# Moving a normalising multiply to GpSimd and charging more transfers in a build-time schedule

## The chip, the cores and the metric

The kernel runs on one core of a Trainium2 chip. The metric is the device time in microseconds (us) of one execution. The profile also gives a span, from the first to the last instruction, which here is about 1.8 us shorter than the time. A run also has a mean granted clock of TensorE, 1.0 being full speed.

The engines: TensorE (PE in the profile) multiplies matrices, ScalarE (ACT) evaluates exponentials, VectorE (DVE) and GpSimd (POOL) do elementwise work, SyncE (SP) issues transfers (DMA).

## The reference, cut to what matters

Two identical layers on an input of 2048 rows and 512 columns in bfloat16. Attention has 32 heads of size 16, so the number of exponentials is large against the size of the matrix products; the feed-forward part has 1792 hidden columns.

```python
def _A_ref(x, wqkv, wo):                      # attention
    ...
    scores = einsum("bhqd,bhkd->bhqk", q, k) * Dh ** -0.5     # 32 heads, 2048 x 2048 each
    p = softmax(scores)
    o = einsum("bhqk,bhkd->bhqd", p, v)
    return o.reshape(B, S, D) @ wo

x = x + _A_ref(layernorm(x), wqkv, wo)
x = x + silu(layernorm(x) @ w1) @ w2
# ... and both lines once more
```

## The kernel before

The kernel is one long stream. In each step TensorE makes four blocks of scores of 128x512 (128 keys by 512 queries). ScalarE takes the exponential of three of them (one instruction on 128x1024, tile `s_ps`, and one on 128x512). The fourth block, `d_ps`, is turned into an exponential without ScalarE: VectorE scales it into 16-bit integers `d_y` that are read as fp16 numbers, and GpSimd adds two offsets to a pair of such blocks, giving `d_z`. Then TensorE multiplies probabilities with values. `d_ps` has one PSUM buffer, so a late evacuation by VectorE holds up the next step's scores, and so ScalarE.

All other work (projections, layernorm, transposes by DMA, feed-forward, head outputs) is background work. It is fitted into the stream when the program is built, by a small model of the engines' clocks:

```python
class Model:
    EXP1 = 0.48          # exponential of 128x512
    EXP2 = 0.905         # of 128x1024
    TRANSPOSE = 1.27     # what one DMA transpose occupies of the queue
    TRANSPOSED = 1.7     # from there until the model counts it as landed
    DMA = 0.64           # what one plain load occupies of the queue
    ...
    def pool_busy(self, us):
        self.pool = max(self.pool, self.dve + 0.1) + us
        return self.pool + 0.1
    def transpose(self):
        self.sp = max(self.sp, self.dve + 0.1) + self.TRANSPOSE
        self.landed = self.sp + self.TRANSPOSED
    def fits(self, cost, landed=0.0):
        held, pe, dve, sums, _ = cost
        if landed > (self.pe if pe else self.dve):
            return False
        ...
```

A part of background work is put in where `fits` says yes; engines then execute in that order whatever the real times are. If the model believes a transfer has landed and it has not, the engine that waits for it holds up everything behind it in its queue.

The output of a head is normalised at its end. For 45 of 64 groups it comes by a DMA transpose (`ot`), for the other 19 through TensorE and PSUM (`att`). Both are then multiplied by the reciprocal of the sums on VectorE:

```python
nc.vector.reciprocal(rec[:], att[:, :, :, 16:17])
yield part(0.43, held=not by_dma(L, qc, pi, g, par))   # the model charges 0.43 us
nc.vector.tensor_tensor(out=attn[...], in0=att[:, :, :, 0:DH],
                        in1=rec[:].to_broadcast([P, 4, 4, DH]), op=ALU.mult)
```

The layernorm result `xn` is also made on VectorE, one 128x513 piece at a time, and transposed by DMA (`xnT`, `fT`):

```python
nc.vector.tensor_scalar(out=wide..., in0=x_wide[...], scalar1=mv[:, 0:1], scalar2=rstd,
                        op0=ALU.subtract, op1=ALU.mult)
```

Before the stream lies a prologue of 14 us (load, layernorm of the first rows, first projection), behind it a tail of 41 us.

The softmax here doesn't subtract the row's maximum and nothing guards it: scores larger than these inputs give would overflow.

## Time and profile before

Three runs took 1565.21 to 1566.28 us, median 1565.61 us. The first view is the one of the cores, the second the head of the page (busy time of each engine, its share of the span, number of instructions).

```profile
core 0: 1562.4 us, clock 0.993
```

```profile
span 1562.4 us, 34354 instructions
PE 1474.8 (94%) x13400; PEld 468.1 (30%) x13400; DVE 1079.3 (69%) x1733; ACT 1513.8 (97%) x2191; POOL 1114.4 (71%) x1184
```

ScalarE is the bound. An exponential of 128x1024 that follows directly behind another instruction ends 0.917 us after it, one of 128x512 0.490 us after it. 1026 + 1032 + 98 (the tanh of the feed-forward) of them make about 1495 us. The stream ran from 14.12 to 1521.5 us. So ScalarE lost only some 13 us inside the stream. (Lost time is counted here from the end of one exponential to the end of the next, less 0.917 or 0.490 us; the cut-off for small waits moves a trace's sum by about 0.4 us. The mean durations in the views below are longer than these figures, because the records of exponentials that follow each other overlap.) It follows that no change that leaves the exponentials alone can win more than these and a little of the prologue.

| where ScalarE waited in the trace of before | us |
|---|---|
| start of the stream, 30 to 45 us | 3.0 |
| 86 us | 1.5 |
| 253 to 256 us | 4.1 |
| 239, 269, 457, 554, 644, 1053 to 1055, 1207 us, each about 3 to 3.5 us behind the start of a slow head-output multiply | 3.5 |
| small ones | 1.0 |

The groups of instructions by shape show the work in question (columns: busy us, mean ns of one; then idle time before them and what ended it).

```profile
L1157 ACT ACTIVATE p_sb<-s_ps 128x512 bf16<-128x512 f32 x1013 | 901.6, 890 | 9.3 <-PE d_ps L925 8.2 <-PE s_ps L925 1.1
L619 DVE TENSOR_TENSOR attn<-ot,rec 128x256 bf16<-128x256 bf16 x45 | 49.4, 1098 | 1.5
L619 DVE TENSOR_TENSOR attn<-att,rec 128x256 bf16<-128x256 f32 x19 | 8.0, 421 | 0.4
L414 DVE TENSOR_SCALAR xn<-x,mv,rstd 128x513 bf16<-128x513 bf16 x64 | 41.6, 663 | 5.7 <-DMA fT<-xn 4.3 <-POOL rstd L408 1.3
```

The same multiply takes 421 ns when its data is in PSUM (`att`) and 1098 ns when both inputs are in SBUF (`ot`), and the model charges 0.43. The timeline shows one of them (start us, duration us, engine, line, instruction; in brackets the idle time before and what ended it).

```profile
453.63 1.04 POOL L1094 TENSOR_SCALAR d_z_7582<-d_y 128x1024 uint16<-128x1024 uint16 x1 [1.39 <-DVE rec L617]
453.67 1.28 DVE L619 TENSOR_TENSOR attn<-ot,rec 128x256 bf16<-128x256 bf16 x1
454.87 0.67 DVE L668 SCALAR_TENSOR_TENSOR hT<-t_sb,h_ps 128x512 bf16<-128x512 f32 x1
...
455.69 0.59 PE L480 MATMUL h_ps<-fT,w_7504 128*128 128x512 bf16 x2 [1.31 <-DVE hT L668]
...
456.68 1.51 ACT L1157 ACTIVATE p_sb<-s_ps 128x512 bf16<-128x512 f32 x2 [0.42 <-PE d_ps L925]
```

The multiply starts 0.04 us after a GpSimd `d_z` and is held until that ends; the evacuation `hT` behind it is late, TensorE waits 1.31 us for it, and ScalarE in the end loses 0.42 us. The largest single loss has another cause, a transfer that landed late:

```profile
246.69 5.58 SPq L317 DMA_TRANSPOSE fT<-xn  x3
...
250.63 0.42 DVE L414 TENSOR_SCALAR xn<-x,mv,rstd 128x513 bf16<-128x513 bf16 x1 [4.13 <-DMA fT<-xn]
...
251.70 0.37 PE L925 MATMUL d_ps<-QT,KT 32*128 32x512 bf16 x1 [3.15 <-DVE d_y L1074]
...
253.44 1.51 ACT L1157 ACTIVATE p_sb<-s_ps 128x512 bf16<-128x512 f32 x2 [3.00 <-PE d_ps L925]
```

VectorE stood 4.13 us in front of an `xn` whose buffer was still being read by an earlier transpose; `d_y` stood behind it, the next `d_ps` behind that, and ScalarE waited 3.00 us.

### The profile page before, as it was taken

The numbers are of one execution on the slowest core, as the hardware profiler recorded it, in microseconds if no ns is written. First come the engines' busy times: TensorE is split into PE (matmuls) and PEld (weight loads), VectorE is DVE, ScalarE is ACT, GpSimd is POOL, SyncE is SP. The second block draws the span as 40 slices with busy tenths as digits, with TensorE's granted clock in tenths as the row PEclk, the third lists the DMA queues.
The fourth block names the chain that finished last, engine by engine and source line by source line (L and its number), as shares of the span: only waits on it lengthen the run. The fifth ranks groups of instructions, "written<-read, shape, count | busy, mean of one in ns | idle before, by whom it ended". The sixth has DMA issues, their size and how long they took to land. (4 is left out here: it accounts for less than half of the span.)

```text
span 1562.4 us, 34354 instructions
## 1 busy us (share of the span) xinstructions
PE 1474.8 (94%) x13400; PEld 468.1 (30%) x13400; DVE 1079.3 (69%) x1733; ACT 1513.8 (97%) x2191; POOL 1114.4 (71%) x1184
## 2 busy tenths in 40 slices
PE   7999998899999999899998999998999899999998
PEld 3222332232322322222322323322332232222225
DVE  6877676667776777767776677676667666676645
ACT  6999998999999999999999999999999999999993
POOL 2888776677876778667876778776777677776760
PEclk9999999999999999999999999999999999999999
DMA  4110023101221112201122010121022101121110
GB/s 142 28 28 2 5 39 62 31 18 42 45 45 28 31 25 49 52 17 41 21 47 45 11 35 8 25 58 32 18 46 62 30 19 29 45 48 22 39 45 14
DMA packets 149443, 55.85 MB, mean 36 GB/s; under 512 B 127776, under 2 KB 148768, under 8 KB 149280
## 3 DMA queue, kind: packets, MB, share of 16 engines
q1 hardware_dynamic: 149280, 53.65, 15.0%
q8 instruction: 105, 1.72, 0.5%
q14 instruction: 58, 0.48, 0.1%
HBM read 28.57 MB, written 4.19 MB: 21 GB/s over the span
## 5 line engine op out<-in xcount | busy, mean ns | idle before, releaser
L1157 ACT ACTIVATE p_sb<-s_ps 128x512 bf16<-128x512 f32 x2026 | 1468.6, 1105 | 9.3 <-PE d_ps L925 8.2
L1074 DVE TENSOR_SCALAR d_y<-d_ps 128x512 uint16<-128x512 f32 x1012 | 696.9, 689 | 400.5 <-PE d_ps L925 359.5
L925 PE MATMUL s_ps<-QT,KT 32*128 32x512 bf16 x3084 | 629.8, 383 | 51.6 <-ACT p_sb L1157 38.8
L925 PE MATMUL d_ps<-QT,KT 32*128 32x512 bf16 x1012 | 390.1, 385 | 10.3 <-DVE d_y L1074 7.1
L925 PEld LDWEIGHTS <-KT 32*128 32x128 bf16 x4096 | 186.8, 91 | 639.9 <-issue 587.1
L949 PE MATMUL o_ps<-p_sb,VA 128*32 128x512 bf16 x3039 | 311.8, 388 | 8.2 <-DVE oB L1054 1.1
L949 PE MATMUL o_ps<-d_y,VA 128*32 128x512 f16 x1012 | 153.2, 379 | 0.0
L949 PEld LDWEIGHTS <-VA 128*32 128x32 bf16 x4096 | 86.7, 95 | 161.6 <-issue 123.8
L727 PE MATMUL f_ps<-w_sb,hT 128*128 128x512 bf16 x392 | 104.1, 382 | 0.0
L949 PEld LDWEIGHTS <-VB 128*32 128x32 f16 x2024 | 78.3, 98 | 55.6 <-issue 0.8
L949 PE MATMUL o_ps<-w_qkv,zero 128*32 128x512 bf16 x1344 | 93.1, 382 | 0.0
L665 ACT ACTIVATE t_sb<-h_ps 128x512 f32<-128x512 f32 x98 | 88.1, 899 | 0.0
L668 DVE SCALAR_TENSOR_TENSOR hT<-t_sb,h_ps 128x512 bf16<-128x512 f32 x98 | 67.2, 686 | 22.8 <-ACT t_sb L665 22.6
L619 DVE TENSOR_TENSOR attn<-ot,rec 128x256 bf16<-128x256 bf16 x45 | 49.4, 1098 | 1.5
L1054 DVE CAST oT<-o_ps 128x512 bf16<-128x512 f32 x64 | 43.5, 680 | 7.7 <-PE o_ps L949 7.7
L414 DVE TENSOR_SCALAR xn<-x,mv,rstd 128x513 bf16<-128x513 bf16 x64 | 41.6, 663 | 5.7 <-DMA fT<-xn 4.3
L403 DVE BATCH_NORM_STATS2 st<-x 128x6 f32<-128x512 bf16 x64 | 43.5, 680 | 2.0 <-DMA x<-in_A_x_dram 2.0
L727 PEld LDWEIGHTS <-hT 128*128 128x128 bf16 x392 | 29.3, 98 | 46.4 <-issue 25.0
L949 PEld LDWEIGHTS <-zero 128*32 128x32 bf16 x1344 | 25.5, 95 | 40.3 <-issue 28.1
L480 PE MATMUL k_ps<-xnT,w_qkv 128*128 128x512 bf16 x128 | 35.4, 389 | 1.6 <-DVE xnT L444 0.9
L480 PE MATMUL q_ps<-xnT,w_qkv 128*128 128x512 bf16 x136 | 36.6, 389 | 0.0
L407 POOL TENSOR_SCALAR rstd<-mv 128x2 f32<-128x2 f32 x32 | 7.7, 240 | 39.4 <-DVE mv L405 37.9
(2299 smaller groups left out, 2109.1 us busy)
## 6 DMA issues: line engine op xcount, KB each, us to landing
wo<-in_A_wo_dram SPq DMA_DIRECT2D x8, 512.0 KB, 3.7
QT<-q SPq DMA_DIRECT2D x240, 16.0 KB, 1.8
x<-in_A_x_dram SPq DMA_DIRECT2D x7, 512.0 KB, 4.3
out_dram<-x SPq DMA_DIRECT2D x16, 128.0 KB, 1.7
w_sb<-in_B_w_dram SPq DMA_DIRECT2D x1, 1792.0 KB, 12.4
w_qkv<-in_A_wqkv_dram SPq DMA_DIRECT2D x3, 512.0 KB, 5.8
w_tail<-in_B_w_dram SPq DMA_DIRECT2D x3, 512.0 KB, 5.2
ot<-oT SPq DMA_TRANSPOSE x45, 2.4
```

Of the source, the lines that this page charges most:

```text
L403: nc.vector.bn_stats(st[:], x_sb[c][:, i, :])
L414: nc.vector.tensor_scalar(out=wide[:].rearrange("p (a b) -> p a b", b=19), in0=x_wide[c][:, D * i : D * (i + 1) + 1], scalar1=mv[:, 0:1], ...
L480: nc.tensor.matmul(ps.rearrange("p (t q) -> p t q", q=P) if len(r.shape) == 3 else ps, lhsT=lhs(ct), rhs=r, start=(ct == 0), stop=(ct == C ...
L619: nc.vector.tensor_tensor(out=attn[L, qc][:, :, P * g : P * (g + 1)].rearrange("p t (j s) -> p t j s", s=32)[:, :, :, 16 * par : 16 * par ...
L665: nc.scalar.activation(t_sb, h_ps, ACT.Tanh, scale=0.5)
L668: nc.vector.scalar_tensor_tensor(out=hT[:, ft, :], in0=t_sb, scalar=1.0, in1=h_ps, op0=ALU.add, op1=ALU.mult)
L727: nc.tensor.matmul(y_ps, lhsT=hT[:, ft, tq * P : (tq + 1) * P], rhs=w2_sb[:, ft, :], start=(ft == 0), stop=(ft == FT - 1),)
L925: nc.tensor.matmul(out, lhsT=KT[L, kt // 4][r, g, (kt % 4) * P : (kt % 4 + 1) * P], rhs=QT[g][r, par, :], start=True, stop=True,)
L949: nc.tensor.matmul(o_tiles[key][32 * j : 32 * j + 32, :], lhsT=lhsT, rhs=rhs, start=(o_count[key][j] == 0), stop=stop,)
L1054: nc.vector.tensor_copy(out=o, in_=o_tiles[key][:])
L1074: nc.vector.tensor_scalar(out=pr["y"][:, len(pr["ds"]), :], in0=s_ps[:], scalar1=float(1024 * SCALE * math.log2(math.e)), scalar2=float(10 ...
L1157: nc.scalar.activation(p_sb, s_ps, ACT.Exp, bias=-SHIFT * math.log(2.0) + math.log(EXP_SUM), scale=float(SCALE),)
```

## The change

It has four parts. (1) The prologue uses the stream's PSUM tiles, transposes tile by tile, and lets ScalarE copy the first keys, so no change of PSUM pools lies ahead of the first scores. (2) The model counts a DMA transpose as landed after 2.4 instead of 1.7 us, charges every load through a helper, and from step 128 on puts in a `d` term only when the model has it ready. (3) The 45 multiplies of transposed heads go to GpSimd, charged 0.62 us there. (4) In the early steps with four score blocks, TensorE gets extra dummy matmuls ("fill") ahead of the late `d` block, meant to keep its clock up; the built program has 2, 5 and 2 of them.

```diff
-    TRANSPOSED = 1.7
+    TRANSPOSED = 2.4
...
+    def load(out, in_):
+        nc.sync.dma_start(out, in_)
+        if bg.model:
+            bg.model.dma(1)
...  (all loads now go through load())
+        copy = nc.scalar.copy if (L, c, g) == (0, 0, 0) else nc.vector.tensor_copy
+        copy(out=KT[L, c][:, g, :], in_=k_ps)
...
-        yield part(0.43, held=not by_dma(L, qc, pi, g, par))
-        nc.vector.tensor_tensor(
+        if by_dma(L, qc, pi, g, par):
+            scale = nc.gpsimd.tensor_tensor
+            bg.model.scaled = bg.model.pool_busy(0.62)
+        else:
+            yield part(0.43, held=True)
+            scale = nc.vector.tensor_tensor
+        scale(
...
+        bg.model.sp = max(bg.model.sp, bg.model.scaled)      # in out_proj
...
-            while d["rhs"] and (must or d["rhs"][0][0] <= t):
+            while d["rhs"] and (
+                must or d["rhs"][0][0] <= t and (t < 8 * NKT or d["ready"][d["rhs"][0][1]] <= m.pe)
+            ):
...  (prologue)
+        for i, tag in ((0, "s1"), (2, "sd")):
+            t_ps = psum["s"].tile([P, 1024], BF16, name="t_ps", tag=tag, bufs=1)...
+            for u, copy in enumerate((nc.scalar.copy, nc.vector.tensor_copy if i else nc.scalar.copy)):
+                xn = ln_apply(0, i + u, mv[:, u, :], rstd[:, u, :])
+                for ct in range(CT):
+                    nc.tensor.transpose(t_ps[:, u, ct, :], xn[:, ct * P : (ct + 1) * P], ident[:, :])
+                copy(out=xnT[0, 0][:, i + u, :, :], in_=t_ps[:, u, :, :])
...
             if n1 == 2 and d_blks:
+                if t > 5 and m.free <= m.pe and bg.idle():
+                    n = int((m.sd - m.pe - 2 * m.SWITCH) / m.GROUP)
+                    if n > 0:
+                        warm(n)
+                        m.to("B")
+                        m.pe += m.GROUP * n
                 m.late_d()
                 emit_d(t, d_blks[0])
```

More of the change, by code (lines that the diff above doesn't have):

```diff
@@ L135, in __init__ @@
         self.mode = None
+        self.scaled = 0.0
         self.early = False
@@ L285 @@
     RUNS += [(1, qc, 0, ORDER, range(NKT)) for qc in range(2, NC)]
+    bg = Background()
     const = ctx.enter_context(tc.tile_pool(name="const", bufs=1))
@@ L328, in load_x @@
         for i in range(0, 4, n):
-            nc.sync.dma_start(x_sb[c][:, i : i + n, :], src[:, i : i + n, :])
+            load(x_sb[c][:, i : i + n, :], src[:, i : i + n, :])
     load_x(0, parts=2)
@@ L354 @@
     nc.scalar.activation(table[:, 0:32], zero[:], ACT.Exp)
-    bg = Background()
     xnT = {}
@@ L500, in proj_k @@
         )
-        nc.vector.tensor_copy(out=KT[L, c][:, g, :], in_=k_ps)
+        copy = nc.scalar.copy if (L, c, g) == (0, 0, 0) else nc.vector.tensor_copy
+        copy(out=KT[L, c][:, g, :], in_=k_ps)
     def proj_q(L, c, g):
@@ L516, in proj_q @@
             for par in range(2):
-                if par == 1 and g == 0:
-                    nc.scalar.activation(
-                        QT[g][:, par, :], q_ps, ACT.Copy, scale=masks[par][:, 0:1]
-                    )
-                    return
                 nc.vector.tensor_scalar_mul(
@@ L647, in load_wo @@
         wo[0] = hpool.tile([P, FT, 512], BF16, name="wo", tag="hT")
-        nc.sync.dma_start(wo[0][:, 0:CT, :], A_wo.rearrange("(ct p) e -> p ct e", p=P))
+        load(wo[0][:, 0:CT, :], A_wo.rearrange("(ct p) e -> p ct e", p=P))
     def out_proj(L, qc):
@@ L681, in ffn_out @@
         tt = 4 * c + i
-        nc.sync.dma_start(of[tt * P : (tt + 1) * P, :] if L == 1 else x1[c][:, i, :], x_sb[c][:, i, :])
+        load(of[tt * P : (tt + 1) * P, :] if L == 1 else x1[c][:, i, :], x_sb[c][:, i, :])
     class W1:
@@ L694, in load @@
                 self.tiles[ft] = w1pool.tile([P, CT, P], BF16, name="w1", tag="w1")
-                nc.sync.dma_start(
+                load(
                     self.tiles[ft][:],
@@ L701, in get @@
             self.load(ft + 2)
-            if bg.model:
-                bg.model.dma(1)
             return self.tiles.pop(ft)
@@ L1082, in emit_d @@
         d = dict(blk=blk, pair=len(pairs), left=NT)
+        d["ready"] = [m.dve + 0.1]
         d["rhs"] = [(t + 1, 0, pr["y"][:, len(pr["ds"]), :].bitcast(FP16))]
@@ L1101, in other_terms @@
             )
-            bg.model.pool_busy(bg.model.ADD[n])
+            ready = bg.model.pool_busy(bg.model.ADD[n])
             for i, d in enumerate(pr["ds"]):
                 d["rhs"].append((t + 3 + k, k + 1, z[:, i, :].bitcast(FP16)))
+                d["ready"].append(ready)
     def end_group(L, qc, pi, g, par):
@@ L1122 @@
     ):
-        with psum_whole("a"):
-            w_ps = bank("warm")
-            for i in range(56):
-                nc.tensor.matmul(w_ps[:, 0:P], lhsT=ident[:], rhs=ident[:], start=True, stop=True)
-            new_v(0, 0)
-            xnT[0, 0] = xslot(0, "xnT")
-            ln = [run(ln_stats(0, (i, i + 1))) for i in (0, 2)]
-            for i in (0, 2):
-                mv, rstd = ln[i // 2]
-                xns = [ln_apply(0, i + u, mv[:, u, :], rstd[:, u, :]) for u in range(2)]
-                ln_transpose(i, xns, xnT[0, 0], nc.vector.tensor_copy if i else nc.scalar.copy)
-            bg.done["ln", 0, 0] = 0.0
-            bg.add(("k", 0, 0, 0), proj_k(0, 0, 0))
-            bg.add(("q", 0, 0, 0, 0), proj_q(0, 0, 0))
-            bg.ensure(("q", 0, 0, 0, 0))
         stream_psum = ExitStack()
         stream_psum.enter_context(psum_stream())
+        early[0] = True
+        w_ps = psum["s"].tile([P, 2, 512], FP32, name="warm", tag="s2", bufs=2)[:, 0, :]
+        for i in range(56):
+            nc.tensor.matmul(w_ps[:, 0:P], lhsT=ident[:], rhs=ident[:], start=True, stop=True)
+        new_v(0, 0)
+        xnT[0, 0] = xslot(0, "xnT")
+        ln = [run(ln_stats(0, (i, i + 1))) for i in (0, 2)]
+        for i, tag in ((0, "s1"), (2, "sd")):
+            mv, rstd = ln[i // 2]
+            t_ps = psum["s"].tile([P, 1024], BF16, name="t_ps", tag=tag, bufs=1)[:].rearrange(
+                "p (u c q) -> p u c q", c=CT, u=2
+            )
+            for u, copy in enumerate((nc.scalar.copy, nc.vector.tensor_copy if i else nc.scalar.copy)):
[3 more added lines that the diff above has]
+                copy(out=xnT[0, 0][:, i + u, :, :], in_=t_ps[:, u, :, :])
+        bg.done["ln", 0, 0] = 0.0
+        bg.add(("k", 0, 0, 0), proj_k(0, 0, 0))
+        bg.add(("q", 0, 0, 0, 0), proj_q(0, 0, 0))
+        bg.ensure(("q", 0, 0, 0, 0))
         for g in range(1, NG):
```

## The prediction

> **What bounds the kernel.** ScalarE. The page gives it 1513.8 us busy of 1562.4. From its records: an exponential of 128x1024 behind another instruction ends 0.917 us after it, one of 128x512 and a tanh 0.490 us. 1026, 1032 and 98 of them make 1495 us; the stream of exponentials runs from 14.1 to 1521.5 us, so ScalarE loses about 13 us inside it. Before it lies a prologue of 14.1 us, behind it a tail of 41 us, which the change leaves alone. VectorE (69%), GpSimd (71%) and TensorE matter only where they make an exponential wait. Everything the change can win is those 13 us and a piece of the prologue: 0.9%.
>
> **Where the 13 us are** (timeline and chain of waits): cold start of the stream, 32 to 45 us, 3.0 us, with matmuls of 0.58 us instead of 0.38; 86 to 90 us, 1.7 us; 239 us 0.3 us; 253 to 256 us, 4.1 us, where VectorE waited 4.1 us in "xn" for the transfer "fT<-xn" and delayed the d_ps evacuations; 269, 456, 554, 644, 1052 to 1055 and 1207 us, together 3.2 us, at least four of them just behind a head-output multiply "attn<-ot" of 1.28 us; small ones.
>
> **Steps, costed.**
> 1. Multiplies to GpSimd: VectorE loses 45 x 1.098 = 49 us of busy time. 37 of the 45 took 1.17 to 1.29 us, the others about 0.42, and the slow ones run together with a GpSimd d_z of 1.04 us. That agrees with the Trainium skill, "SBUF — State Buffer", "Who interferes with whom": a VectorE instruction with two SBUF inputs contends with a GpSimd one that reads SBUF, and one fully blocks. On GpSimd I estimate 0.45 to 0.9 us each (its 128x1024 takes 1.04 us, 136 elements 0.30), 20 to 40 us more busy, GpSimd to 73%. Critical part: most of the 3.2 us, about 2.5.
> 2. Model charges transfers and landing 2.4 instead of 1.7: the fourth "xn" moves behind the next pieces of the stream (the built order shows it 4 steps later), so the 4.4 us at 239 to 256 us should go, and feed-forward matmuls come a few steps later, which ScalarE doesn't notice.
> 3. Early fill: the built order has 9 extra matmuls (2, 5, 2) in the three four-block steps at 33 to 38 us; otherwise that stretch is unchanged. Saves part of the cold 2.4 us: 1.0. The page "TensorE: Matmul & The Clock Gate", "Part 1", says a window of about 3.4 us decides the clock, so it may not suffice. The 86 us stall is left: order there is unchanged, and its cause (two "xn" of 1.2 us blocked by d_z) stays.
> 4. Prologue: no pool change ahead of the first scores, which now wait only for the first masked Q (12.86 instead of 13.58). But the built waits make transposes 2 and 4 wait for the copy of the other half of their PSUM tile, so the projection starts an estimated 0.6 to 0.9 later. Net 0, within 0.3.
> 5. New collisions: +0.5.
>
> Sum: 2.5 + 4.4 + 1.0 - 0.5 = 7.4 us off: 1558.2 us, range 1554 to 1562. Faster by over 2%: 0.005; within 2%: 0.985; slower by over 2%: 0.01.
>
> **What would show it.** No "attn" on VectorE; GpSimd "attn<-ot" 0.45 to 0.9 us; VectorE's wait for "fT<-xn" near 256 us gone; ScalarE stalls in the stream about 5.5 us; exponentials starting at 14.1 +- 0.3 us; tail 41 us.
>
> **What would make it wrong.** The multiply slow on GpSimd and d_z late for TensorE; VectorE's "xn" and GpSimd blocking each other more often; fills that push score matmuls late; a prologue that loses a microsecond; deferred work piling up before the tail.

## More of the kernel before

The view of windows gives, for two stretches, busy time (and instructions) of PE, PEld, DVE, ACT and POOL, then the granted clock, the DMA share and GB/s:

```profile
29.00:46.00 17.00, 13.07 (x90) 2.39 (x87) 13.24 (x26) 14.71 (x22) 9.68 (x13) 0.70 0.26 64
250.00:258.00 8.00, 6.30 (x49) 1.58 (x48) 4.52 (x8) 4.10 (x7) 3.34 (x4) 0.79 0.23 49
```

ScalarE was busy for only 4.10 of 8 us around 254 us, and TensorE's clock was below full in both stretches.

## The result, and the profile after

Six runs of after took 1557.28 to 1564.65 us, median 1561.28; six of before beside them 1564.36 to 1567.12, median 1565.58. The ratio is 0.9973 with a 95% interval of 0.9955 to 0.999: a small gain, well inside 2%. A ratio here is not quite the ratio of the medians quoted (the furthest apart is model_only, 1.0035 against 1.0052).

```profile
core 0: 1555.5 us, clock 0.999
```

```profile
span 1555.5 us, 34303 instructions
PE 1467.6 (94%) x13299; PEld 475.1 (31%) x13397; DVE 1033.7 (66%) x1688; ACT 1513.3 (97%) x2193; POOL 1138.7 (73%) x1229
```

```profile
L1174 ACT ACTIVATE p_sb<-s_ps 128x512 bf16<-128x512 f32 x1013 | 935.9, 924 | 2.0 <-PE d_ps L932 1.8
L421 DVE TENSOR_SCALAR xn<-x,mv,rstd 128x513 bf16<-128x513 bf16 x64 | 39.8, 634 | 2.8 <-POOL rstd L415 1.3 <-DMA xnT<-xn 0.8 <-DMA fT<-xn 0.6
L627 POOL TENSOR_TENSOR attn<-ot,rec 128x256 bf16<-128x256 bf16 x45 | 27.9, 620 | 0.0
```

VectorE lost 45.6 us of busy time and GpSimd gained 24.3; neither was the bound. The multiply takes 620 ns on GpSimd, in all 45 cases (0.62 us each), and GpSimd stood idle before none of them. ScalarE's wait for `d_ps` ahead of the 128x512 exponentials fell from 8.2 to 1.8 us, VectorE's wait for `fT<-xn` from 4.3 to 0.6 us. The same two stretches as before:

```profile
29.00:46.00 17.00, 13.10 (x104) 3.00 (x108) 13.82 (x27) 15.62 (x24) 10.27 (x14) 1.00 0.31 64
250.00:258.00 8.00, 7.70 (x86) 2.17 (x79) 5.24 (x9) 8.00 (x13) 5.59 (x7) 1.00 0.42 82
```

At 250 to 258 us ScalarE is now busy for all 8.00 us. But a wait is there that before did not have in this size. The first line is the same matmul in before, the others are from after:

```profile
451.31 1.04 PE L480 MATMUL h_ps<-fT,w_7423 128*128 128x512 bf16 x4 [0.24 <-DMA w_7423<-in_B_w_dram]
```

```profile
442.99 1.22 SPq L320 DMA_TRANSPOSE ot<-oT  x1
...
444.25 0.58 SPq L325 DMA_DIRECT2D w_7456<-in_B_w_dram  x1
...
446.92 1.04 PE L487 MATMUL h_ps<-fT,w_7456 128*128 128x512 bf16 x4 [1.68 <-DMA w_7456<-in_B_w_dram]
...
448.00 0.60 ACT L674 ACTIVATE t_sb<-h_ps 128x512 f32<-128x512 f32 x1 [0.87 <-PE h_ps L487]
```

TensorE waited 1.68 us for a feed-forward weight whose load was issued only at 444.25 us, behind a transpose; ScalarE lost 0.98 us there. The same at 636 us cost 0.79 us. Summed over the stream, ScalarE lost 13.1 us in the trace of before and 6.6 in that of after. The first exponential came at 13.76 instead of 14.12 us.

This trace has the highest clock of the first six runs of after, and it is the fastest of them. The six spans ran from 1555.5 us at clock 0.999 to 1562.9 us at 0.993. So one trace of after is not enough; both kernels were run again.

### The profile page after: what moved, and what is told of

It is laid out like the page before. It is cut to its first block, busy times and chain, and to the rows that moved or that the text cites. A ratio compares the mean times of both kernels' runs of the same rounds, so it can differ in the third digit from the quotient of the medians.

```text
span 1555.5 us, 34303 instructions
## 1 busy us (share of the span) xinstructions
PE 1467.6 (94%) x13299; PEld 475.1 (31%) x13397; DVE 1033.7 (66%) x1688; ACT 1513.3 (97%) x2193; POOL 1138.7 (73%) x1229
## 5 line engine op out<-in xcount | busy, mean ns | idle before, releaser
L932 PE MATMUL s_ps<-QT,KT 32*128 32x512 bf16 x3084 | 646.5, 380 | 51.7 <-ACT p_sb L1174 37.8
L932 PEld LDWEIGHTS <-KT 32*128 32x128 bf16 x4096 | 192.6, 91 | 647.9 <-issue 599.5
L734 PE MATMUL f_ps<-w_sb,hT 128*128 128x512 bf16 x350 | 97.1, 382 | 3.9 <-issue 3.2
L487 PE MATMUL v_ps<-w_qkv,xnT 128*128 128x512 bf16 x112 | 33.0, 382 | 1.7 <-issue 0.6
```

The source lines that it names most:

```text
L487: nc.tensor.matmul(ps.rearrange("p (t q) -> p t q", q=P) if len(r.shape) == 3 else ps, lhsT=lhs(ct), rhs=r, start=(ct == 0), stop=(ct == C ...
L734: nc.tensor.matmul(y_ps, lhsT=hT[:, ft, tq * P : (tq + 1) * P], rhs=w2_sb[:, ft, :], start=(ft == 0), stop=(ft == FT - 1),)
L932: nc.tensor.matmul(out, lhsT=KT[L, kt // 4][r, g, (kt % 4) * P : (kt % 4 + 1) * P], rhs=QT[g][r, par, :], start=True, stop=True,)
```

## The experiments

Twelve more runs were made, all correct; two of them are the unchanged kernels. They came in four batches, each on one chip with before timed beside it: the first four rows of the table (chip 3, median of before 1564.86 us), the next four (chip 3, 1564.67), best_a and best_b (chip 14, 1565.17), best_no_fill and mult_24 (chip 15, 1564.94). Across batches, compare the ratios.

| kernel | median us (range) | ratio to before [95%] | what it has |
|---|---|---|---|
| before_again | 1566.56 (1565.23 to 1568.83) | 1.0004 [0.9988, 1.0021] | nothing changed |
| after_again | 1561.13 (1559.23 to 1565.40) | 0.9969 [0.9951, 0.9988] | the whole change |
| model_only | 1572.97 (1567.90 to 1574.69) | 1.0035 [1.0015, 1.0056] | part 2 |
| mult_only | 1569.65 (1566.98 to 1570.30) | 1.0020 [1.0003, 1.0036] | part 3 |
| model_mult | 1561.54 (1559.58 to 1562.65) | 0.9977 [0.9965, 0.9989] | parts 2 and 3 |
| after_no_fill | 1562.65 (1561.59 to 1565.68) | 0.9988 [0.9976, 1.0000] | all but part 4 |
| after_17 | 1566.21 (1563.99 to 1572.48) | 1.0013 [0.9995, 1.0031] | all, landing at 1.7 |
| after_w1 | 1560.81 (1558.17 to 1563.33) | 0.9972 [0.9959, 0.9984] | all, and feed-forward gated by its weights |
| best_a | 1555.62 (1555.14 to 1556.68) | 0.9938 [0.9926, 0.9951] | see below |
| best_b | 1579.55 (1577.80 to 1581.93) | 1.0090 [1.0076, 1.0104] | best_a, and a charge for held `xn` |
| best_no_fill | 1556.21 (1555.85 to 1557.59) | 0.9940 [0.9928, 0.9952] | best_a without its fills |
| mult_24 | 1559.54 (1558.89 to 1560.44) | 0.9961 [0.9949, 0.9973] | part 3 and landing 2.4 alone |

### Both kernels again

No edit. The theory was the prediction's: the gain is the sum of waits removed. The rival was that a part of the difference between two traces is TensorE's clock, which falls differently in each run.

> The kernel before, unchanged, for the clock of each of its runs and a second trace. In its first trace the TensorE clock was halved in six windows of 3.41 us (three from 34.28 us, one each from 85.5, 252.7 and 1051.5 us). Theory A (the long waits decide): the windows follow the idle stretches of TensorE, which are in the program, so every run has about the same clock, 0.993 to 0.994, and 1564 to 1567 us. Theory B (luck of the phase): the number of halved windows differs from run to run by two or more and the span follows it by about 1.2 us a window.

> The kernel after, unchanged, for a second trace and more pairs of span and clock. Its six runs so far spread from 1557.3 to 1564.7 us, with the clock from 0.999 to 0.993. Theory B (phase of the clock's windows): the spread comes back, the spans lie on one line against the clock, 1.2 us for each 0.001, and a trace of a slow run shows halved windows and waits of ScalarE at places where the first trace has none. Theory A (a difference of the chip or of the day): all runs of this job lie within 2 us of each other.

```profile
core 0: 1567.1 us, clock 0.989
```

```profile
core 0: 1560.2 us, clock 0.995
```

The first of these is before_again, the second after_again. The difference of the traces is 6.9 us again, yet both are 4.7 us longer than the first pair. The first two traces have 6 halved-clock windows of 3.41 us in the stream of before and 1 in that of after, the repeats 10 and 5: four more each, about 1.2 us a window, as theory B has it. In before_again, ScalarE lost 17.5 us; 3.9 of them at 933 us, where the first trace of before lost nothing:

```profile
930.37 1.87 PE L480 MATMUL k_ps<-xnT,w_qkv 128*128 128x512 bf16 x4 [1.89 <-DMA xnT<-xn]
...
932.85 1.51 ACT L1157 ACTIVATE p_sb<-s_ps 128x512 bf16<-128x512 f32 x2 [2.49 <-PE d_ps L925]
```

The program is the same; here the last of the four transposes took 4.13 us to land and came too late for the projection, there it took 2.44 us. Why it took longer is not known. In after_again the fills themselves did harm. First the view of windows of after_again, then its timeline, then the same fill in the first trace of after:

```profile
29.00:46.00 17.00, 13.60 (x79) 2.45 (x75) 12.04 (x24) 13.12 (x20) 7.93 (x12) 0.80 0.29 64
```

```profile
33.04 1.04 PE L765 MATMUL warm<-w_qkv,ident 128*128 128x512 bf16 x2
...
35.15 0.60 ACT L1174 ACTIVATE p_z<-s_ps 128x512 bf16<-128x512 f32 x1 [1.41 <-PE s_ps L932]
...
35.91 2.31 PE L765 MATMUL warm<-w_qkv,ident 128*128 128x512 bf16 x5
...
39.32 1.22 ACT L1174 ACTIVATE p_z<-s_ps 128x512 bf16<-128x512 f32 x2 [1.80 <-PE s_ps L932]
```

```profile
34.32 1.25 PE L765 MATMUL warm<-w_qkv,ident 128*128 128x512 bf16 x5
...
36.24 0.60 ACT L1174 ACTIVATE p_z<-s_ps 128x512 bf16<-128x512 f32 x1 [0.31 <-PE s_ps L932]
```

Five fills took 1.25 us at full clock and 2.31 at half clock. They were given a hole that fits them at full clock; at half clock the scores come late behind them and ScalarE waits 1.80 instead of 0.31 us. The stretch from 30 to 50 us cost ScalarE 2.1 us in after, where the clock never fell, and 4.6 in after_again, where it fell from 32.2 to 39.1 us. Over all traces in which the clock fell for three or more windows at the start, the stretch cost 3.0 to 3.9 us without any fill (seven traces, three or four windows) and 7.2 with the early fill (after_17 and after_w1, five windows).

Over the twelve runs of after in both batches the span goes with the granted clock: 1555.5 us at 0.999, and 0.91 us more for each 0.001 less (a fitted line, correlation -0.94). Part of that is the stalls lowering the clock and part the clock lengthening the stalls; the fit does not separate them. The range of 8 us of the same program is as large as the whole gain predicted.

### Part 2 and part 3 alone and together

model_only is before with the landing time, the charges of loads and the gate on `d` terms. mult_only is before with the multiply on GpSimd. Their core edits are the lines of part 2 and part 3 in the diff above, nothing else. model_mult has both; it is after without parts 1 and 4.

The theory was that the parts remove different waits, so their gains add: the multiply alone wins its 2.5 us, the model its 4.4. The rival was that both edit one schedule, so each shifts the rest and the gains need not add.

> Before, with only the model's part of the change (landing 2.4, every load charged, terms held until the model has them ready); multiplies still on VectorE, old prologue, no early fill. By the prediction's step 2: the wait at 253 to 256 us goes and nothing else, 4.4 us off, about 1561.2 us; the multiplies of 1.28 us still make ScalarE wait, in sum about 3 us. The rival: the model's part gives nothing of its own (under 1 us), as loads charged late are issued late and TensorE then waits for weights.

> Before, with only the head-output multiplies moved to GpSimd (with their charge in the model). By the prediction's step 1: 2.5 us off, about 1563 us; the wait at 253 us stays. The rival: the multiplies' blocking was hidden, the waits behind them came from the halved clock, and the time stays within 1 us of before.

> The model's part and the multiplies on GpSimd together, without early fill and with the old prologue: the fourth corner beside before (1564.9 us), the model's part alone (1571) and the multiplies alone (1568). If the parts only add up, this one must be the slowest, 1571 + 1568 - 1565 = 1574 us. If each is worth something only with the other (the model packs VectorE's queue by 0.43 us a multiply where it really takes 1.28 beside GpSimd; on GpSimd it takes the 0.62 that the model charges), it is near after, 1561 to 1563 us, with no halved clock window behind a multiply.

Neither won alone: model_only lost 0.35% and mult_only 0.20%, the latter only just clear of noise (before_again, the same program, had an interval up to 1.0021). Together they won 0.23%. The parts do not add. In model_only, the wait at 253 us is gone, but the multiplies are still on VectorE and many more of them now stand ahead of a wait of ScalarE (the clock of the whole trace was 0.986):

```profile
447.73 1.28 DVE L626 TENSOR_TENSOR attn<-ot,rec 128x256 bf16<-128x256 bf16 x1
...
449.75 1.01 PE L487 MATMUL h_ps<-fT,w 128*128 128x512 bf16 x2 [1.06 <-DVE hT L675]
...
451.37 1.51 ACT L1166 ACTIVATE p_sb<-s_ps 128x512 bf16<-128x512 f32 x2 [0.81 <-PE d_ps L930]
...
453.30 1.51 ACT L1166 ACTIVATE p_sb<-s_ps 128x512 bf16<-128x512 f32 x2 [0.41 <-PE d_ps L930]
```

This is the chain of before at 456 us over again, with a second wait behind it: TensorE ran at half clock (its two matmuls took 1.01 instead of 0.59 us). Fourteen multiplies of 1.27 to 1.28 us have ScalarE waiting within 5 us of their start, against seven slow ones in before. That the loss needs the multiplies on VectorE is shown by model_mult, in which only they and their charge differ and which is 11.4 us faster. Not all of the loss lies behind them, though: 2.4 us at 568 to 570 us follow a wait of TensorE for `xnT`. Why the shifted schedule meets `d_z` so unluckily was not tested.

In mult_only no wait lies behind a multiply. But the model still counts 1.7 us, and 3.1 us are lost behind a late transpose at 252 to 255 us. Another 1.2 us at 453 and 1.3 at 642 to 644 us are behind late weights (TensorE waited 1.88 and 1.34 us for them). A late transpose is behind the largest new one:

```profile
747.13 1.86 PE L481 MATMUL k_ps<-xnT,w_qkv 128*128 128x512 bf16 x4 [2.14 <-DMA xnT<-xn]
...
749.61 1.51 ACT L1164 ACTIVATE p_sb<-s_ps 128x512 bf16<-128x512 f32 x2 [2.73 <-PE d_ps L932]
```

My reading is that taking 45 x 0.43 us of charge off the modelled VectorE let background work run closer to transfers whose landing was counted too early. Whether the landing figure decides it, the next runs test.

### The landing time

after_17 is after with one number put back, mult_24 is mult_only with one number changed.

```diff
# after_17 against after
-    TRANSPOSED = 2.4
+    TRANSPOSED = 1.7
```

```diff
# mult_24 against mult_only
-    TRANSPOSED = 1.7
+    TRANSPOSED = 2.4
```

The theory was that 2.4 us removes the waits for transposes near 253 and 750 us. For after_17 the rival was that the charges of loads do, for mult_24 that the multiply in GpSimd's queue, ahead of `d_z`, is what makes mult_only slow.

> After with one number put back: the model takes a transposed tile as landed 1.7 us after its issue, not 2.4. If that number is what takes away the waits for transfers (DVE xn for fT<-xn, PE k_ps for xnT<-xn, each 2 to 4 us with one or two halved windows), some come back here and the time rises by 2 to 5 us, to 1563 to 1566 us. If charging the loads and the multiplies did it, the time stays within 1 us of after.

> mult_only (1569.7 us) with the model's landing of a transposed tile put at 2.4 us instead of 1.7, and nothing else. If mult_only is slow because work that was packed more tightly ran into transposed tiles that had not landed (in its trace 3.1 us near 252 and 2.8 us near 750, both behind a wait for xnT or fT), those go and the time falls by 4 to 7 us, to 1563 to 1566 us. If it is slow because the multiply sits in GpSimd's queue ahead of the d_z, the time stays within 2 us of 1569.7.

after_17 lost the whole gain (1.0013), with ScalarE losing 2.0 us at 257 us and 1.7 at 750 us again. The first of these in its trace:

```profile
253.08 0.42 DVE L421 TENSOR_SCALAR xn<-x,mv,rstd 128x513 bf16<-128x513 bf16 x1 [1.84 <-DMA fT<-xn]
...
256.72 0.60 ACT L1174 ACTIVATE p_sb<-s_ps 128x512 bf16<-128x512 f32 x1 [1.53 <-PE d_ps L932]
```

Another 7.2 us of its trace's 16 were the start, with the clock down; after_w1, which counts 2.4, lost the same there, so that part is not the landing figure's. mult_24, without any other part of the change, is at 0.9961, as good as the whole change or better (their intervals overlap). So the multiply on GpSimd and this one number, together, are enough to give what the change gives; model_mult, which has the charges of loads and the gate on `d` terms as well, is no better (0.9977). The rival for mult_only is out: the time fell by 10.1 us (by the ratios about 9), more than the 4 to 7 expected. Only these two values were tried, and every edit of the model shuffles the whole order, so that 2.4 is in part a lucky order is not excluded. Whether 2.4 with the multiply left on VectorE loses alone, as model_only does, was not run.

What the number means, the list of transfers in the profile tells. There the landing counts from the start of the issue. The model's total from there is 1.27 + 1.7 = 2.97 us with the old number and 1.27 + 2.4 = 3.67 us with the new one. The 45 `ot<-oT` and the 28 `fT<-xn` of before took a median of 2.4 and 2.5 us, which the old number covers. But of the four `fT<-xn` between 244 and 254 us, issued while a load of 512 KB and two of 128 KB were under way, the first two took 5.2 and 4.4 us (the other two 2.4), and of the four `xnT<-xn` ahead of the wait at 747 us in mult_only the second and third took 4.4 and 3.8. So the new number is no better a median, and it does not cover these transposes either; it is a margin that puts the work behind them later in the order. It is not a full one: mult_24 still lost 1.1 us at 253 us.

### The fills, and the weights

after_no_fill is after without the lines of part 4. after_w1 makes the feed-forward wait in the model until a weight tile has landed, 2.05 us after the modelled end of its issue, read off the trace of after:

```diff
# after_w1 against after
+                bg.done["w1", ft] = bg.model.sp + 2.05        # in W1.load
...
         for ft in range(FT):
+            yield part(need=("w1", ft))
             w = w1.get(ft)
```

> After without the early fill alone. By the prediction's step 3 the fill is worth 1.0 us: about 1562.3 us here. The rival, from the second trace of after, where the clock was halved from 32.2 us and the fills of twice the length held up the scores (two waits of 1.5 and 1.9 us): the fill gives a little in some runs and takes more in others, so this kernel is within 1 us of after, or faster.

> After, and the model lets a feed-forward matmul begin only when its weights have landed (2.05 us after the modelled issue). This aims at the new waits of after: TensorE waiting 1.8 to 2.0 us for weights near 448 and 636 us, 1.6 us of ScalarE's time in the first trace and 3.9 us in the second, where one brought two halved windows. Expected 1.5 to 3 us off after: 1558 to 1560 us, with no wait of TensorE over 1 us for a weight tile. The rival: the waits only move, as the work is pushed later and collides elsewhere, within 1 us of after.

after_no_fill: 1562.65 us, 0.9988; the interval overlaps that of after in either batch, so the fill's worth is not shown, and the estimate of 1.0 us is neither confirmed nor refuted. As after_no_fill is also model_mult plus part 1 (0.9977), no worth of the new prologue is shown either; in its trace the first exponential came only at 16.00 us, with TensorE at half clock from 11.1 to 14.5 us. In the same trace the clock fell from 35 to 49 us and the stretch cost 3.8 us, between after's 2.1 (clock up) and after_again's 4.6 (clock down).

after_w1: the waits at 448 and 636 us are gone from its trace, as the theory said; what remained of size was the start (7.2 us, the clock down from 32.7 to 49.8 us) and 1.6 us at 90 to 94 us. Its time, 1560.81 us, is not told apart from after's. In the traced run the start took back what the gate gave; the other runs have no trace.

Either part alone already brings a wait for weights: the longest of TensorE near 450 us was 1.88 us in mult_only, 1.56 in mult_24, 1.96 in model_mult, 1.68 in after and 0.24 in before; model_only has none there, but one of 1.61 us at 642 us. In all of them the model knew nothing of when a weight tile lands.

### What puts the clock down

Inside the stream, halved-clock stretches in all traces last 3.41 us or a multiple of it, and in one trace all their starts have the same phase modulo 3.413 us; from run to run the phase differs (0.15 us in before, 2.26 in after, 1.33 and 1.53 in the repeats). This agrees with the Trainium skill, "TensorE: Matmul & The Clock Gate", "Part 1: The HAM clock gate", which says that TensorE's activity is judged in free-running windows of 3413 ns. The page says that the clock falls after at least one idle window. Here no window needed to be idle: in mult_only a wait of 2.14 us at 745 to 747 us was followed by a halved window, in model_only one of 1.06 us at 449 us. From 14 traces I counted, for each such window at full clock between 16 and 1520 us, the share in which TensorE streams, and whether the next window was halved. A matmul of 512 columns is taken to stream for 0.213 us from its start (in after, those that follow each other directly start 0.216 us apart), and matmuls that overlap are counted once:

| streaming share of the window | next window halved |
|---|---|
| under 0.40 | 16 of 16 |
| 0.40 to 0.45 | 24 of 29 |
| 0.45 to 0.50 | 6 of 16 |
| 0.50 to 0.55 | 5 of 15 |
| 0.55 to 0.60 | 1 of 38 |
| 0.60 and over | 0 of 5964 |

So a wait of TensorE of some 2 us may or may not cost a halved window, depending on how it falls into the windows. As a halved window also makes waits longer, removing a wait can be worth more than its length in one run and not in another. The table is a count over traces of these kernels, not an experiment that sets the share.

### A version that beats both

best_a is after with the gate on weights, with each of the first four transposes in a PSUM tile of its own, and with the early fill replaced by fills between the two single score blocks, where the scores wait for ScalarE anyway. best_no_fill is best_a without those last fills. best_b is best_a with a charge in the model for an `xn` that is held by GpSimd.

```diff
# best_a against after (besides the edit of after_w1)
+                home, tag = (("m", "m"), ("o", "o"), ("s", "s1"), ("s", "sd"))[i + u]
+                t_ps = psum[home].tile([P, 1024], BF16, name="t_ps", tag=tag, bufs=1)[:, 0:D]...
...
             for i in range(n1):
+                if i == 1 and pairs and not fill(2) and bg.idle():
+                    warm(2)
                 score(a_blks[i], s1[i])
...
-                if t > 5 and m.free <= m.pe and bg.idle():      # the early fill, taken out
-                    ...
# best_b against best_a, in the layernorm
+                if bg.model and bg.model.pool > bg.model.dve - 0.45:
+                    bg.model.dve = max(bg.model.dve, bg.model.pool + 0.15)
```

> After with the weights' gate of after_w1 and two more edits. (1) The early fill is put where TensorE waits in any case 0.57 us or more for the evacuation of the bank it writes next (between the two single score blocks), two matmuls each, instead of up to five ahead of the d block: if low use of TensorE in one window of 3.41 us is what halves the clock there, the windows between 29 and 43 us stay over 0.5 and ScalarE loses 2 to 3 us at the stream's start instead of 7.1 (after_w1); if the fills cost more than they save, it loses as much as without them, 3.7. (2) Each of the four first transposes gets a PSUM tile of its own: the first exponential 0.5 to 1.0 us earlier than the 13.8 to 14.1 us of after; the rival is that it waits for something else (weights for the keys) and gains nothing. In sum 1554 to 1557 us, clock 0.996 or higher.

> best_a, and the model knows that a normalisation step (xn) on VectorE that meets a GpSimd d_z ends only 0.15 us after that d_z. If the wait near 86 us (1.0 to 1.9 us in every trace so far) comes from two xn in a row that were blocked, it goes here: 1 to 1.5 us off best_a. The rival: the order is shuffled and other waits appear, within 1 us of best_a or slower.

> best_a without its eight groups of fill matmuls and nothing else changed: the work of ScalarE, VectorE and GpSimd and its order are the same. If the share of a 3.41 us window in which TensorE streams decides its clock, windows at 29 to 35 us fall to 0.46 to 0.53 in every phase, the clock is halved there in most runs (four windows, clock 0.993 to 0.995), ScalarE loses about 3.7 us there instead of 2.1 to 3.1, and the median is 1 to 3 us above best_a, 1556.5 to 1558.5 us, with a wider spread of the runs. If the fills are only cost or only luck, it is at best_a's 1555.6 us or below.

best_a took 1555.62 us, 0.9938, and its six runs lie within 1.6 us of each other, where after's lay within 7.4 and 6.2. ScalarE lost about 5.0 us in its trace (after: 6.6 and 10.8). One part of it is visible in the prologue, first in before, then in after, then in best_a:

```profile
13.63 0.40 PE L925 MATMUL s_ps<-QT,KT 32*128 32x512 bf16 x4 [1.56 <-ACT QT L518]
14.12 1.02 ACT L1157 ACTIVATE p_pre<-s_ps 128x1024 bf16<-128x1024 f32 x1 [0.54 <-PE s_ps L925]
```

```profile
9.64 0.38 PE L1151 MATMUL t_ps<-ident,xn 128*128 128x128 bf16 x4 [0.87 <-ACT xnT L1152]
...
10.61 1.02 PE L487 MATMUL k_ps<-xnT,w_qkv 128*128 128x512 bf16 x4 [0.58 <-DVE xnT L1152]
...
13.76 1.94 ACT L1174 ACTIVATE p_pre<-s_ps 128x1024 bf16<-128x1024 f32 x2 [1.51 <-PE s_ps L932]
```

```profile
9.99 1.02 PE L487 MATMUL k_ps<-xnT,w_qkv 128*128 128x512 bf16 x4 [0.61 <-DVE xnT L1155]
...
13.15 1.02 ACT L1177 ACTIVATE p_pre<-s_ps 128x1024 bf16<-128x1024 f32 x1 [1.51 <-PE s_ps L934]
```

In after, the fourth transpose waits 0.87 us for ScalarE's copy of the other half of the same PSUM tile, and the projection starts at 10.61 us; with own tiles it starts at 9.99 us, and the first exponential comes at 13.15 instead of 13.76 us.

best_no_fill, at 1556.21 us, is not told apart from best_a, the medians differ by 0.6 us, so a worth of the new fills in time is not shown. Their clock is a little higher (0.996 to 0.998 in best_a's runs, 0.995 or 0.996 without the fills), but in best_a's trace it was halved at 38.5 to 45.3 us all the same, and the stretch from 30 to 50 us cost 2.8 us against 3.0. The gain of best_no_fill over after came from the gate, the prologue's tiles and the absence of the early fill; how it divides among these was not measured. best_b is a clear miss: with the honest charge, the layernorm and the keys of layer 1 came later than the step that needs them, and ScalarE waited 4.87 us at 943.7 and 7.28 at 964.3 us. A further try, to charge the multiply on VectorE at its true 1.28 us without moving it, could not be built: an out-projection was then no longer done when the next one came due.

## Why the prediction was right or wrong

The range held the result (1561.28 in 1554 to 1562), the direction and the class were right, and so was the bound: ScalarE's busy time is 1513.8 before and 1513.3 us after, and the gain came out of its waits. The centre, 1558.2, promised 7.4 us and the medians show 4.3. That the sum came so near owes something to luck: neither of its two large terms was won by its part alone.

- Step 1, the multiply. Right in what it named: 0.62 us on GpSimd (0.45 to 0.9 predicted), GpSimd at 73%, and no wait behind a multiply in either trace of after. Its reading of the hold-up is confirmed as far as these runs go: the Trainium skill, "SBUF — State Buffer", "Who interferes with whom", says that a VectorE instruction with two SBUF inputs contends with a GpSimd one that reads SBUF; here it is 1.28 us against 0.42 with one input in PSUM, and 11 of the 19 multiplies of that kind ran wholly beside a `d_z` and took 0.42 all the same. Wrong as a separate gain of 2.5 us: alone, the move made the kernel 0.2% slower.
- Step 2, the model. The wait at 253 us went, as predicted and in the way predicted (4.1 us in before, none in either trace of after; the fourth transpose is issued at 256.3 instead of 251.1 us), and after_17, where 2.0 us came back at 257 us, shows that the landing figure did it. Wrong as a separate gain of 4.4 us: part 2 alone made the kernel 0.35% slower.
- Step 3, the fill, 1.0 us. Not shown. The prediction's own doubt, that the window of 3.4 us decides, was the right one: of two traces of after, the clock fell at the start in one and not in the other, and where it has fallen, the fill delays the scores. That the phase of the windows decides it is my reading; no run sets the phase.
- Step 4, the prologue, 0 within 0.3 us. The first exponential came 0.36 and 0.25 us earlier in the two pairs of traces, the first just outside; the wait for the other half of the PSUM tile was there as read from the built order.
- The 86 us stall was to stay, and stayed: 1.5 us in before, 1.6 and 1.8 in the two traces of after.
- Step 5, "New collisions: +0.5". This term of the sum was too small. The new waits in the traces of after (weights at 448 and 636 us, one of 0.43 us at 373 us) cost 2.2 us, and 3.6 in after_again (0.8 + 2.24 + 0.54), so 1.7 to 3.1 us more than allowed. That is near the 3 us by which the centre missed, but it is not shown to be the cause. The traced run of after has 2.2 us of these waits and still took 1557.28 us, less than the centre; both pairs of traces differ by 6.9 us; and after_w1, without the waits for weights, is not told apart from after. The medians lie nearer together than the traces, and the span of after goes with the clock its runs were granted, 0.999 in the traced one and 0.993 to 0.997 in the five others. What the median would be without the new waits stays open. The order of instructions showed the feed-forward moving; that its weights would be late could have been computed from its weights' place in the queue, and was not.

Two premises under the sum failed as well. The prediction added the gains of parts that edit one schedule; the four corners (before 1, model 1.0035, multiply 1.0020, both 0.9977) show that they do not add. And it took the waits of one trace for those of the program: before's own traces differ by 4.4 us of lost time, after's by 4.2.

## What to carry to other kernels

Where a schedule is fixed at build time by a model, an optimistic figure for when a transfer lands costs waits wherever transfers meet, and freeing an engine moves work into new places of that kind (the 2.8 us at 750 us of mult_only); so measure the landing times and correct them in the same change that frees an engine, and test the parts in pairs as well as singly. Fill put in front of work that the bound engine waits for is a bet on the clock; it belongs where the next instruction must wait anyway. When a gain of a few microseconds is read from two traces, take a second pair first: here the same program gave 4.7 us of difference between its own traces.

## What the Trainium skill lacked or had wrong

- "TensorE: Matmul & The Clock Gate", "Part 1: The HAM clock gate": says the clock falls after at least one idle window. Here windows that were far from idle were followed by a halved one: all 16 below a streaming share of 0.40, 24 of 29 from 0.40 to 0.45, and none of 5964 at 0.60 and above. The page has no such threshold, though elsewhere it tells, also without a number, of a kernel whose clock went up and down on short but frequent idle times.
- The same page, "HAM oscillation — how this bites in real kernels", gives as its rule that TensorE should not idle for more than about 3.4 us. Here waits of 1.06 and 2.14 us were enough. And the page tells of the luck of the window's phase only for the kernel's start; here it seems to bear on what a stall in mid-kernel costs as well: twelve runs of one program spread from 1557.28 to 1565.40 us, the span going with the granted clock.
- "SBUF — State Buffer", "Who interferes with whom": says that a VectorE instruction with at most one SBUF input, outside the 2-port modes, does not contend with GpSimd. Here `xn`, a tensor_scalar with one 16-bit SBUF tensor and two per-partition scalars, took 0.41 us alone and in before up to 1.24 beside a GpSimd `d_z`, ending 0.15 us after it in 35 of its 64 cases. The page lists tensor_scalar among those that can enter such a mode; whether this one did, no run here shows, so this is a case to look at and not an error that was shown.
- "DMA: Bandwidth & Descriptors", "Anatomy of one DMA — SWDGE (gpsimd) path", has a fixed part of about 2.0 us for a transfer issued from GpSimd. For a DMA transpose issued from SyncE, as a scheduler needs it, I found no time from issue to landing ("VectorE: DVE Perf Modes", "The three transpose paths", has one time for a 128x128 block, without saying from where to where); here it was a median of 2.4 us for 128x512, and up to 5.2 us beside other loads.
